# A gated linear recurrence and a low-rank mixer on one core: 96 packed rows for 112, first logarithms summed on TensorE, the sign from bits, and another order

## The chip, the core and the metric

The kernel runs on one core of a Trainium2 chip. The metric is device time in microseconds (us), the median of repeated runs. The core has five engines with queues of their own: TensorE (PE; its weight loads are listed as PEld), VectorE (DVE), ScalarE (ACT), GpSimd (POOL) and SyncE (SP, which issues most DMAs). [...]

## The reference, cut to what matters

```python
# q, k, v, a_re, a_im: (4 batches, 8 heads, 768 steps, 48), float32
mag = np.sqrt(a_re * a_re + a_im * a_im)
scale = np.minimum(mag, 0.999) / (mag + 1e-06)
ar, ai = a_re * scale, a_im * scale
for t in range(S):                       # a state of 48 x 48 complex numbers per head
    new_re = ar[t] * S_re - ai[t] * S_im
    new_im = ar[t] * S_im + ai[t] * S_re
    S_re, S_im = new_re + outer(k[t], v[t]), new_im
    y[t] = q[t] @ S_re
x = y as (4, 768, 384)                   # heads side by side
u = x + (x.transpose(0, 2, 1) @ U @ V).transpose(0, 2, 1)      # rank 32 over the 768 steps
out = u + np.maximum(u @ w_ch1, 0) @ w_ch2                     # 384 -> 1536 -> 384
```

U, V and the two weight matrices come as float64 and are turned into float32 on the chip.

## The kernel before, in words

**Chunks.** Each batch's 768 steps are six chunks of 128, so there are 24 chunks (0 to 23; chunk 5 is the last of the first batch). The complex gates are kept as a logarithm of the magnitude and an angle. Sums of these over the steps of a chunk are products of a 0/±1 matrix with them on TensorE, and exponentials, sines and cosines of the sums turn q and k so that the recurrence becomes products of q with k inside a chunk and a state that goes from chunk to chunk.

**Gates.** Chunks go in groups of two (0 to 11). For a group, `magnitudes_of` (from line 629) takes squares, logarithms and exponentials on ACT and combines them on DVE: `l` is the logarithm of the normalised magnitude, made of two parts, a capped −0.5 ln and a correction `y`. Group 0 is done chunk by chunk (tiles of 384 columns), the others at once (768). `within` sums `l` over the steps (`es ps` and `ef ps`, lines 692 and 696), `of_blocks` over blocks (`tot`, lines 735 and 741). For groups 3 to 11 (`SPLIT`) `l` is split into two rounded parts, `GS`, each with a product of its own in the fp32r format, one record in the trace; for groups 0 to 2 it is one product in float32, which the trace shows as two records. `turns_of` and `angles` (from line 752) make the angle from an arctangent and the sign of a_re. For groups 0 to 2 the sign, times 1/pi, is made on DVE from a_re's bits, and the added 1/4 comes from a product with a constant column; for groups 3 to 11 ACT's Sign function and an Identity with scale 1/pi and bias 1/4 do it (line 384 is the helper through which all activations are recorded; lines 387 and 390 record DVE's products and sums).

**Prep and chain.** `prep` weighs q and k, multiplies them by cosine and sine into `QKC`, per head two parts of 48 columns in 64 each, of which the first 112 of 128 columns are used (48 real, 16 zeros, 48 imaginary), turns them by transposes (line 860, 16 per q or k, in pairs on two halves of the rows) and copies them to `QK` with 112 rows. `chain` scales `QK` by the block totals `T` and takes products over those 112 rows: `inner` (907, 910), `corners` (971), the state's part `dk` (996) and the outputs `y` (1027, 1035), which ACT copies to `xo` (1044, 1046). `T`'s sixteen unused rows are set to one at the start.

**Mixer.** After a batch's six chunks, `mixer` takes two chunks at a time (mixers 0 to 11): rank sums (1070), their spread onto xo (1089), transposes (1107), the products with the first matrix (`up`, 1122; from mixer 7 on `few`, 1222, a scheme with fewer products) and with the second (`down`, 1313 for mixer 0, 1356 from mixer 1 on). Mixer 0's ups are taken before the rank sums are known and put right afterwards (`put_right`, `fix`, 1161). The weights are decoded on DVE and ACT (`single`, 573 to 580).

**Order.** Nothing is scheduled by the compiler. Every operation is first recorded with a kind (such as ("DVE", "gates")); the table `ORDER` then gives each one a place in one global list, found by a planner outside the kernel, and each engine gets its operations in the order of that list. A second table, `SPARE`, gives places at which `idle` (line 1519 records it) puts up to so many blocks of 128 columns of a product of the identity with itself into a PSUM tile that is free at that moment: **filler**, with no use for the result, where the planner expects TensorE to wait.

Of the kernel before, what the change touches and what calls it, by code (L numbers as in the profile page):

```python
# [19 lines left out]
HC = CH // 2  # L20
# [19 lines left out]
        ("POOL", "load"): {0: [14], 1: [34], 1.5: [84], 2: [31]},  # L40
        ("DVE", "load"): {1: [58]},
# [199 lines left out]
def kernel(  # L241
# [19 lines left out]

    nc = tc.nc
    B, H, S, D = q.shape
    DP = 64
    DQ = DP + D
    DM = H * D  # L270
    FF = moe_w_ch1.shape[1]
    R = moe_U.shape[1]
    KD = DM // 128
# [78 lines left out]
    def c_one(n):  # L352
        return 0.15 + 0.00052 * n
# [1235 lines left out]
```

## Time and profile before

| | before |
|---|---|
| median of 3 runs | 628.74 us (627.27 to 629.45) |
| span of the profiled execution | 627.0 us |
| PE / PEld busy | 609.9 / 526.2 us |
| DVE / ACT busy | 499.7 / 415.8 us |
| POOL busy | 38.1 us |
| mean granted TensorE clock | 0.995 |
| filler (line 1519) on PE | 30.6 us |

The span goes from the first to the last instruction of one profiled execution. Busy time of PE is the time in which at least one matmul is under way; an engine's busy time doesn't tell whether its work sets the end. Slices and stages tell more: early stages are about supply, later ones about TensorE's own work.

### The profile page before, as it was taken

The page shows a single profiled execution, that of the slowest core. Times are in us where ns is not written, and L with a number is a line of the kernel's source. Part 1 is how long each engine was busy: PE and PEld are TensorE (multiplying, and loading weights), DVE is VectorE, ACT ScalarE, POOL GpSimd, SP SyncE. Part 2 cuts the span into 40 slices and gives each one's busy share as a digit, 9 for nine tenths or more (in the row PEclk, how much of TensorE's full clock was granted, in tenths as well). Part 3 has the DMA queues.
Part 4 walks back from the last instruction along what each step waited for, and adds up shares of the span by engine and source line. Part 5 has one row for each costly group of instructions (what it writes and reads, how often), then busy time and mean ns, then how long its engine had stood idle before and what let it go on. Part 6 is the DMA issues. An engine that isn't in the chain of part 4 may idle for free.

```text
span 627.0 us, 23447 instructions
## 1 busy us (share of the span) xinstructions
PE 609.9 (97%) x10380; PEld 526.2 (84%) x10380; DVE 499.7 (80%) x887; ACT 415.8 (66%) x807; POOL 38.1 (6%) x79
## 2 busy tenths in 40 slices
PE   6998989999999999999999999999999999999998
PEld 3566767666889889889989989888999998999997
DVE  6899999888999979758977867788989884464554
ACT  6999999999898988687787867688433431202010
POOL 5000000000001010010000100000100100000100
PEclk7999999999999999999999999999999999999999
DMA  8864565644143252541512512601203020000101
GB/s 211 191 146 115 135 136 132 155 111 104 33 80 76 50 120 44 99 89 28 99 37 46 113 40 46 124 19 25 63 21 60 9 51 3 1 1 1 45 14 44
DMA packets 173685, 45.74 MB, mean 73 GB/s; under 512 B 167632, under 2 KB 170384, under 8 KB 173584
## 3 DMA queue, kind: packets, MB, share of 16 engines
q1 hardware_dynamic: 171376, 39.90, 30.1%
q0 software_dynamic: 2208, 4.35, 2.1%
q8 instruction: 81, 1.33, 0.9%
q14 instruction: 20, 0.16, 0.1%
HBM read 33.59 MB, written 4.72 MB: 61 GB/s over the span
## 4 chain that ended last, share of the span: by engine, by line
PE 77%; ACT 4%; DVE 3%; DMA 1%; issue 1%; SPq 0%; ACTq 0%; DVEq 0%
PE down L1356 24%; PE up L1122 15%; PE few L1222 11%; PE dk L996 3%; PE tr L860 3%; PE y L1035 3%; PE inner L910 2%; PE down L1313 2%; PE inner L907 2%; PE tot L741 2%; PE y L1027 2%; PE mixed L1089 2%; PE es ps L692 1%; PE ef ps L692 1%; PE uTp L1107 1%; PE corners L971 1%
## 5 line engine op out<-in xcount | busy, mean ns | idle before, releaser
L1122 PE MATMUL up<-uT,w 128*128 128x256 f32 x504 | 116.9, 383 | 0.0
L387 DVE TENSOR_TENSOR QK<-QK,T 112x512 f32<-112x512 f32 (+2 forms) x144 | 102.1, 732 | 8.4 <-PE inner L910 4.3
L1122 PEld LDWEIGHTS up<-uT,w 128*128 128x128 f32 x504 | 93.6, 190 | 12.5
L1356 PE MATMUL down<-w,h 128*128 128x192 f32 x396 | 72.2, 331 | 0.0
L384 ACT ACTIVATE gate<-gate 128x768 f32<-128x768 f32 (+1 forms) x82 | 64.8, 795 | 7.4 <-DVE GS L791 3.2
L1356 PEld LDWEIGHTS down<-w,h 128*128 128x128 f32 x396 | 64.1, 190 | 1.5 <-issue 0.7
L871 ACT COPY QK<-tr 112x512 f32<-112x512 f32 x96 | 51.2, 590 | 14.6 <-PE tr L860 14.3
L390 DVE TENSOR_TENSOR xo<-down,xo 128x192 f32<-128x192 f32 (+1 forms) x79 | 29.9, 387 | 27.5 <-PE down L1356 27.0
L387 DVE TENSOR_TENSOR QKC<-qk,cs 128x768 f32<-128x768 f32 x44 | 41.7, 955 | 6.3 <-ACT cs L384 3.6
L1230 ACT COPY h<-few 128x512 f32<-128x512 f32 x30 | 17.2, 586 | 40.8 <-PE few L1222 40.8
L1356 PE MATMUL down<-stage 128*128 128x192 f32 x198 | 37.6, 331 | 0.0
L1111 ACT COPY uT<-uTp 128x384 f32<-128x384 f32 x22 | 10.0, 479 | 41.4 <-PE uTp L1107 26.9
L1222 PE MATMUL few<-gate,w 128*128 128x128 f32 x280 | 34.8, 275 | 0.0
L1298 POOL DMA_DIRECT2D out_dram<-xo x32 | 19.2, 644 | 243.3 <-DVE xo L390 140.0
L860 PEld LDWEIGHTS tr<-ident,QKC 64*112 64x112 f32 x768 | 24.5, 130 | 10.7 <-issue 4.7
L1222 PEld LDWEIGHTS few<-gate,w 128*128 128x128 f32 x280 | 33.3, 192 | 0.0
L1356 PEld LDWEIGHTS down<-stage 128*128 128x128 f32 x198 | 32.1, 190 | 0.7 <-issue 0.2
L779 POOL DMA_DIRECT2D gate<-F x15 | 12.0, 799 | 327.9 <-DVE w L578 113.5
L860 PE MATMUL tr<-ident,QKC 64*112 64x64 f32 x768 | 29.4, 221 | 2.3 <-DVE QKC L387 1.6
L381 ACT ACT_TABLE_LOAD x24 | 30.8, 1283 | 1.1 <-PEq L1573 0.7
L384 ACT ACTIVATE h<-up 128x512 f32<-128x512 f32 x42 | 24.6, 596 | 9.8 <-PE up L1122 9.5
L976 ACT COPY AT<-corners 32x128 f32<-32x128 f32 x96 | 24.2, 255 | 9.6 <-PE corners L971 8.3
(200 smaller groups left out, 1285.4 us busy)
## 6 DMA issues: line engine op xcount, KB each, us to landing
stage<-in_moe_w_ch_dram SPq DMA_DIRECT2D x12, 768.0 KB, 5.0
qk<-in_q_dram SPq DMA_DIRECT2D x24, 192.0 KB, 3.2
qk<-in_k_dram SPq DMA_DIRECT2D x24, 192.0 KB, 2.7
VP<-in_v_dram SPq DMA_DIRECT2D x24, 192.0 KB, 3.6
gate<-in_a_re_dram SPq DMA_DIRECT2D x22, 192.0 KB, 3.4
gate<-in_a_im_dram SPq DMA_DIRECT2D x22, 192.0 KB, 3.4
AT<-DG SPq DMA_DIRECT2D x96, 32.0 KB, 2.3
T<-E SPq DMA_DIRECT2D x48, 48.0 KB, 2.9
```

What stands on the lines that cost most here:

```text
L381: ACT(1.37, rank, lambda: nc.scalar.preload_act_table_set(name), writes=[TABLE])
L384: return nc.scalar.activation(out=o, in_=i, func=f, **kw)
L387: nc.vector.tensor_tensor(out=o, in0=a, in1=b, op=OP.mult)
L390: nc.vector.tensor_tensor(out=o, in0=a, in1=b, op=OP.add)
L860: nc.tensor.transpose(out=get(*ps[r])[0:DQ, h], in_=get(*qkc)[at, h].rearrange("p u d -> p (u d)")[:, 0:DQ], identity=ident[at, at], tile_ ...
L871: nc.scalar.copy(out=to, in_=a)
L976: ACT(0.36, RR, lambda r=r, u=u: nc.scalar.copy(out=get(*ATi).rearrange("p (a u) t -> p a u t", u=2)[r:r + BLK, :, u, BLK:2 * BLK], in_=ge ...
L996: nc.tensor.matmul(out=get(*dk[r])[x:end, h], lhsT=get(*ks)[at, h, x // DP, 0:end - x], rhs=get(*VPi)[at, h], start=True, stop=True, tile_ ...
L1122: nc.tensor.matmul(out=get(*ps)[:, e], lhsT=w1[:, f, (ff + e) * 128:(ff + e + 1) * 128], rhs=get(*uT)[:, f], start=(f == 0), stop=(f == KD ...
L1222: nc.tensor.matmul(out=get(*ps)[:, q], lhsT=w()[:, q * 128:(q + 1) * 128], rhs=v[0](), start=(n == 0 and q == 0), stop=True, skip_group_ch ...
L1298: queue.dma_start(out=out[b, c * CH:(c + 1) * CH, lo:hi], in_=get("xo", i)[:, lo:hi])
L1356: nc.tensor.matmul(out=get(*to)[:, part], lhsT=x(j), rhs=y[:, j], start=(first and j == 0), stop=(j == KH - 1), skip_group_check=not first)
```

## The change

1. **96 rows.** `QKC`'s real and imaginary columns stand side by side, 96 per head, with no zeros between; transposes, `QK`, `T` and the states have 96 rows in place of 112. `dk` still takes two products per head and half, of 64 and 48 columns, so that it reads 16 columns of the next head, whose rows in PSUM nobody reads. The memsets of `T` go; those of `QKC` shrink to 32 columns.
2. **Logarithms (groups 0 to 2).** The cap is one DVE pass with one input in all three groups (in groups 1 and 2 it was a Relu on ACT and a two-input pass on DVE), and `l` and `y` are no longer added: each sum takes one product with each of them in the same PSUM tile.
3. **Sign from bits (groups 3 to 11).** Sign on ACT becomes the one-input DVE pass; ACT's Identity goes, and the 1/4 is added while the angle is split into its two rounded parts (ACT's cast gets a bias, DVE's subtraction an added constant).
4. **Order.** `ORDER` and `SPARE` are new throughout: 89 blocks of filler, all of which find a free tile, in place of 153, of which 91 found one. Forty of the 89 stand ahead of the first sum, where there were 8.

The numbers of instructions go from 5664 to 5712 on TensorE, from 887 to 893 on DVE, from 783 to 763 on ACT (24 table loads beside them) and from 79 to 76 on POOL. The diff without `ORDER`, cut to its core:

```diff
-SPARE = {20: 8, 32: 9, 62: 1, 66: 1, 73: 1, 82: 5, 91: 1, 113: 6, 116: 1, 119: 8, 140: 8, 153: 6, 157: 4, 167: 1, 168: 1, 207: 6, 216: 1, 217: 1, 282:
-         1, 352: 2, 436: 1, 514: 5, 518: 5, 527: 4, 546: 4, 547: 25, 551: 12, 596: 2, 601: 1, 606: 3, 624: 1, 632: 3, 646: 1, 653: 1, 664: 1, 672: 2,
-         678: 5, 694: 1, 695: 1, 717: 1, 718: 2}
+SPARE = {30: 40, 83: 6, 95: 3, 107: 10, 115: 4, 142: 6, 148: 2, 223: 5, 260: 7, 265: 2, 578: 2, 601: 2}
...
+    DQ = 2 * D
     DP = 64
-    DQ = DP + D
...
-        QKC.append(singles.tile([128, H, 2, DP], FP, name="QKC%d" % n))
-        nc.gpsimd.memset(QKC[n][:, :, :, D:DP], 0.0)
+        QKC.append(singles.tile([128, H * DQ + DP - (DQ - DP)], FP, name="QKC%d" % n))
+        nc.gpsimd.memset(QKC[n][:, H * DQ:], 0.0)
...
-        nc.gpsimd.memset(TS[n], 1.0)
...
-            if on_dve:
+            if g not in SPLIT:
                 DVE(c_one(W), R1, lambda: nc.vector.tensor_scalar(out=t(l), in0=t(l), scalar1=-0.5, scalar2=-LNMAX, op0=OP.mult,
                                                                   op1=OP.max), [], [L])
-                DVE(cd, R1, lambda: add(t(l), t(l), t(y)), Y, [L])
...
-            if g in BITS:
-                DVE(c_one(W), R1, lambda: nc.vector.tensor_scalar(out=t(n).bitcast(U32), in0=t(ar).bitcast(U32), scalar1=0x80000000,
-                                                                  scalar2=INV_PI, op0=OP.bitwise_and, op1=OP.bitwise_or), AR, [N])
-            else:
-                ACT(ca + 0.09, R1, lambda: act(t(n), t(ar), AF.Sign, bias=tiny), AR, [N])
+            DVE(c_one(W), R1, lambda: nc.vector.tensor_scalar(out=t(n).bitcast(U32), in0=t(ar).bitcast(U32), scalar1=0x80000000,
+                                                              scalar2=INV_PI, op0=OP.bitwise_and, op1=OP.bitwise_or), AR, [N])
...
-                    PE(0.65, R1, lambda: nc.tensor.matmul(out=get(*to), lhsT=m.bitcast(FP), rhs=of(l, i), start=True, stop=True),
-                       [L, name], [to, ("sums", g, i)], takes=[keeps], steps=2)
+                    def two():
+                        for u, a in enumerate((y, l)):
+                            nc.tensor.matmul(out=get(*to), lhsT=m.bitcast(FP), rhs=of(a, i), start=(u == 0), stop=(u == 1))
+                    PE(1.3, R1, two, [L, y + (i,), name], [to, ("sums", g, i)], takes=[keeps], steps=4)
...
-                        nc.tensor.matmul(out=get(*ps)[u * 64:u * 64 + w, p], lhsT=get(*l)[:, h:h + w], rhs=total, start=True,
-                                         stop=True, tile_position=(0, u * 64))
+                        for n, a in enumerate((y, l)):
+                            nc.tensor.matmul(out=get(*ps)[u * 64:u * 64 + w, p], lhsT=get(*a)[:, h:h + w], rhs=total, start=(n == 0),
+                                             stop=(n == 1), tile_position=(0, u * 64))
...
-            if g not in BITS:
-                ACT(ca + 0.09, R2, lambda: act(t(z), t(z), AF.Identity, scale=1.0 / math.pi, bias=fourth), [], Z)
...
-                    ACT(c_act(DM), R2, lambda: nc.scalar.copy(out=of(a, i), in_=of(z, i)), [zi], [a + (i,)])
+                    ACT(c_act(DM) + 0.09, R2, lambda: act(of(a, i), of(z, i), AF.Identity, bias=fourth), [zi], [a + (i,)])
...
-                DVE(c_dve(DM), R2, lambda: nc.vector.tensor_tensor(out=of(b, i), in0=of(z, i), in1=of(a, i).bitcast(FP), op=OP.subtract),
-                    [zi, a + (i,)], [b + (i,)])
+                DVE(c_dve(DM), R2, lambda: nc.vector.scalar_tensor_tensor(out=of(b, i), in0=of(z, i), scalar=0.25, in1=of(a, i).bitcast(FP),
+                                                                          op0=OP.add, op1=OP.subtract), [zi, a + (i,)], [b + (i,)])
...
-                        nc.tensor.transpose(out=get(*ps[r])[0:DQ, h], in_=get(*qkc)[at, h].rearrange("p u d -> p (u d)")[:, 0:DQ],
+                        nc.tensor.transpose(out=get(*ps[r])[0:DQ, h], in_=get(*qkc)[at, h * DQ:(h + 1) * DQ],
                                             identity=ident[at, at], tile_position=(r * HC, 0))
...
-                    for x, end in ((0, DP), (DP, DQ)):
-                        nc.tensor.matmul(out=get(*dk[r])[x:end, h], lhsT=get(*ks)[at, h, x // DP, 0:end - x], rhs=get(*VPi)[at, h],
+                    for x, w in ((0, DP), (DP, D)):
+                        nc.tensor.matmul(out=get(*dk[r])[x:x + w, h], lhsT=get(*ks)[at, h * DQ + x:h * DQ + x + w], rhs=get(*VPi)[at, h],
                                          start=True, stop=True, tile_position=(r * HC, x))
```

(The costs in us inside `PE(...)`, `ACT(...)` and `DVE(...)` are what the planner assumed; the kernel itself does nothing with them.)

More of the change, by code (lines that the diff above doesn't have):

```diff
@@ L30 @@
 ORDER = {
[9 rows of a table removed]
-        ("POOL", "load"): {0: [14], 1: [34], 1.5: [84], 2: [31]},
-        ("DVE", "load"): {1: [58]},
[6 rows of a table removed]
-        ("ACT", "gates"): {0: [1, 2, 4, 6, 7, 16, 17, 22, 23, 29, 28, 45, 70, 71], 1: [24, 27, 38, 39, 41, 42, 46, 47, 65, 64, 67, 68], 2: [129, 108,
[10 rows of a table removed]
-        ("DVE", "gates"): {0: [5, 8, 13, 18, 19, 54, 49], 1: [30, 21, 40, 43, 44, 51, 50], 2: [111, 143, 156, 185, 169], 4: [277, 322, 323, 372, 356],
[10 rows of a table removed]
-        ("ACT", "angles"): {0: [72, 86, 98, 100, 103], 1: [76, 106, 112, 114, 126], 2: [210, 231, 251, 240, 241, 242, 263, 269, 271], 4: [375, 395,
[5 rows of a table removed]
@@ new lines @@
+        ('POOL', 'small'): {0: [884, 1093], 1: [1155, 1018, 1064], 2: [1342, 1377, 1398], 3: [1524, 1468, 1498], 4: [1728, 1771, 1772], 5: [1937,
+        1885, 1957], 6: [2168, 2064, 2127], 7: [2387, 2278, 2289], 8: [2532, 2432, 2515], 9: [2533, 2510, 2564], 10: [2631, 2621, 2640]},
+        ('POOL', 'angles'): {6: [602], 8: [710, 751], 10: [861, 903], 12: [1078], 14: [1246, 1271], 16: [1438, 1474], 18: [1662], 20: [1820, 1862],
+        22: [1990, 2026]},
+        ('DVE', 'mixing'): {7: [1981, 2004, 1995, 2042, 2084, 1986, 1988, 2058, 2067, 2072, 2111, 2117, 2051]},
+}
@@ L301 @@
     PL = H * HC
-    BITS = range(SPLIT[0])
     PUT = (0, 2), (4, 6), (8, 10)
@@ L744, in of_blocks @@
             else:
-                PE(0.51, R1, sums, [l, ("total", 0), ("sums", g)], [ps], way=1, takes=[e], steps=4 * HH)
+                PE(0.82, R1, sums, [l, y + (i,), ("total", 0), ("sums", g)], [ps], way=1, takes=[e], steps=8 * HH)
             used = 2 * D if g in SPLIT else 64 + D
```

45 lines of the change are left out of this document (24 added, 21 removed), and 248 rows, old and new, of the table ORDER.

## The prediction

> **What bounds the kernel now.** I read the page first, for the engines' shares and the slices of the span:
>
> ```profile
> PE 609.9 (97%) x10380; PEld 526.2 (84%) x10380; DVE 499.7 (80%) x887; ACT 415.8 (66%) x807; POOL 38.1 (6%) x79
> PE   6998989999999999999999999999999999999998
> DVE  6899999888999979758977867788989884464554
> ACT  6999999999898988687787867688433431202010
> PEclk7999999999999999999999999999999999999999
> ```
>
> TensorE (PE) is busy for 97% of the 627.0 us, so it looks like the bound. Two things qualify that. Some of the busy time is filler: matmuls of the identity (line 1519), which the order puts in where it expects TensorE to wait. And VectorE (DVE) and ScalarE (ACT) are as full as TensorE in the first quarter. So I cut the span into stages. One limit is the moment at which the output of chunk 5, the last chunk of the first batch, has been copied out, since the rest of mixer 0 hangs on it; the timeline puts it at 117.5 us:
>
> ```profile
> 116.52 0.30 ACT L1044 COPY xo<-y 128x192 f32<-128x192 f32 x1
> 116.84 0.64 ACT L1046 COPY xo<-y 64x192 f32<-64x192 f32 x2
> ```
>
> The busy times by stage (stretch, length, then PE, PEld, DVE, ACT, POOL with counts, granted clock, DMA share, GB/s), and below them the filler's share alone (PE, PEld; its third row is a part of its second):
>
> ```profile
> 0.00:20.00 20.00, 14.13 (x61) 8.38 (x62) 13.62 (x37) 13.21 (x26) 8.41 (x32) 0.83 0.89 212
> 20.00:117.50 97.50, 91.00 (x2152) 67.37 (x2151) 95.56 (x150) 94.05 (x184) 0.00 (x0) 1.00 0.60 140
> 117.50:155.00 37.50, 36.20 (x222) 21.83 (x217) 32.17 (x47) 34.73 (x54) 2.50 (x3) 1.00 0.51 123
> 155.00:600.00 445.00, 444.61 (x7786) 404.92 (x7785) 345.98 (x631) 272.68 (x544) 25.01 (x40) 1.00 0.25 50
> 600.00:627.00 27.00, 23.97 (x169) 23.67 (x167) 12.38 (x26) 1.17 (x2) 2.15 (x4) 1.00 0.10 34
> ```
>
> ```profile
> 0.00:20.00 20.00, 8.89 (x18) 5.05 (x18) 0.83 0.89 212
> 20.00:117.50 97.50, 15.00 (x50) 8.75 (x50) 1.00 0.60 140
> 50.00:117.50 67.50, 1.57 (x6) 0.97 (x6) 1.00 0.57 133
> 117.50:155.00 37.50, 6.71 (x24) 3.90 (x24) 1.00 0.51 123
> ```
>
> The reader is to see three regimes. From 155 to 600 us TensorE never rests (444.61 of 445) and there is no filler: every microsecond of TensorE work there is a microsecond of time, and nothing else is. From 20 to 117.5 us DVE (95.56 of 97.5) and ACT (94.05) are full, while TensorE has 91.0 − 15.0 = 76.0 us of real work: it is fed too slowly. From 117.5 to 155 us TensorE has 36.20 − 6.71 = 29.5 us of real work in 37.5, so it waits 8.0 us, idle or behind filler. The real work is 609.9 − 30.6 = 579.3 us, of which 14.1 − 8.9 + 76.0 = 81.2 lie before 117.5 and 498.1 after it. **The span is thus 117.5 + 498.1 + waits of 8.0, 0.4 and 3.0** (117.5 to 155, to 600, to the end) = 627.0. The prediction replaces each of these terms.
>
> **The change, part by part.** Its single instructions first (line, engine, form, count, busy us, mean ns, idle before):
>
> ```profile
> L384 ACT ACTIVATE GL<-GL,lmax 128x768 f32<-128x768 f32 x10 | 9.3, 930 | 0.1
> L384 ACT ACTIVATE gate<-gate,tiny 128x768 f32<-128x768 f32 x9 | 8.4, 938 | 0.0
> L384 ACT ACTIVATE gate<-gate,fourth 128x768 f32<-128x768 f32 x9 | 8.4, 931 | 2.3 <-DVE gate L760 2.1
> L788 ACT CAST GS<-gate 128x384 fp32r<-128x384 f32 x16 | 8.3, 517 | 1.5 <-DMA gate<-F 1.3
> L384 ACT ACTIVATE F<-ph,magic 128x384 f32<-128x384 f32 x24 | 13.9, 579 | 8.2 <-PE ph L796 7.4 <-PE ph L804 0.4 <-PE ph L801 0.3
> L663 DVE SCALAR_TENSOR_TENSOR GL<-GL,gate 128x768 f32<-128x768 f32 x10 | 9.5, 955 | 3.0 <-ACT gate L384 2.9
> L390 DVE TENSOR_TENSOR GL<-GL,gate 128x384 f32<-128x384 f32 x2 | 1.1, 568 | 0.3 <-ACT gate L384 0.2
> L678 DVE TENSOR_SCALAR gate<-gate 128x768 uint32<-128x768 uint32 x1 | 0.6, 559 | 0.0
> ```
>
> *Sign and fourth (groups 3 to 11).* ACT loses nine Sign (938 ns) and nine Identity (931); its sixteen casts gain a bias, 579 for 517 by the nearest row. DVE gains nine one-input passes of 559. In all ACT −15.8 us, DVE +5.0; the subtraction that now also adds the fourth stays one two-input pass.
>
> *Logarithms (groups 0 to 2).* DVE loses two additions of 568 in group 0; groups 1 and 2 trade a Relu on ACT (930) and a 955 pass on DVE for one of 559. TensorE pays, since each sum now takes two products. The start shows their price (start, length, instruction, count; one product is two records):
>
> ```profile
> 1.42 3.58 PE L1519 MATMUL tr<-ident 128*128 128x384 f32 x6 [1.42 <-POOL ident masks.py:199]
> 8.79 1.62 PE L696 MATMUL es ps<-GL,mid 128*128 128x384 f32 x2 [3.79 <-DVE GL L390]
> 10.21 0.34 PEld L1519 LDWEIGHTS tr<-ident 128*128 128x128 f32 x1 [0.30 <-issue]
> 10.85 0.34 PEld L1519 LDWEIGHTS tr<-ident 128*128 128x128 f32 x1 [0.30 <-issue]
> 15.35 0.81 PE L696 MATMUL es ps<-GL,mid 128*128 128x384 f32 x2
> 16.00 0.81 PE L696 MATMUL ef ps<-GL,fore 128*128 128x384 f32 x2
> 17.69 1.09 PE L735 MATMUL tot<-total,GL 128*64 128x32 f32 x32 [0.66 <-ACT es L384]
> 19.13 1.28 ACT L381 ACT_TABLE_LOAD   x1
> ```
>
> Products of 384 columns follow each other at 0.65 us (15.35 to 16.00), and two chunks' totals take about 1.05. So the twelve sums gain 12 × 0.65 = 7.8 us and the six totals 6 × 0.52 = 3.1: **TensorE +10.9 us, all ahead of 117.5**.
>
> *96 rows for 112.* Rows are the partitions that a product contracts over. The shapes that only lose rows keep their columns, and elementwise passes keep their length per partition, so I cost these at nothing. Only the 768 transposes shrink, their loads from 112 columns to 96:
>
> ```profile
> 97.08 1.08 PE tr L860 x32
> L860 PEld LDWEIGHTS tr<-ident,QKC 64*112 64x112 f32 x768 | 24.5, 130 | 10.7 <-issue 4.7
> L1107 PEld LDWEIGHTS uTp<-ident,xo 128*128 128x128 f32 x72 | 9.0, 141 | 1.0 <-issue 0.4
> ```
>
> Sixteen columns are 11 ns between the last two rows. The transposes go in pairs on two halves of the rows, so 384 pairs save between 0 (load hidden) and 4.2 us; some three quarters lie after 117.5. I take −1.9 there, about the middle, with 0 and −3.2 as ends.
>
> [...]
>
> *The start.* Ahead of the first sum stand now 40 blocks of filler (thirteen products of 384 columns and one of 128) where eight stood; the sum used to wait for the logarithm until 8.79 us. At the cold clock such a product takes 1.28 us (weight loads at 10.21 and 10.85, two per product). Before, the clock was slow until about 14.7, 5.9 us after TensorE took up work at 8.8. If filler from 1.42 on also needs 5.9 us, 4.6 products go cold and 8.7 at 0.65: the first sum starts at 13.2; eight products (5.2) and the totals (2.1) end at 20.5 instead of 18.8. All cold gives 25.8. The chain of angles hangs on this: ACT's exponentials of the totals stand ahead of the table load (19.13), and behind it the first arctangents. ACT's queue is held too, and DVE runs out of weights to decode. I take **+1.5 us**, ends 0 and +7.
>
> [...]
>
> *The order.* Counted through the output of chunk 5, the new order has ahead of it, on DVE: −1.1 (two additions), −0.8 (groups 1, 2), +0.6 (group 3's sign), and pulled forward from later 1.3 (group 3's angle) and 2.5 (one block of w2): net +2.4 us. On ACT: −2.8, and 4.5 pulled forward (three decodes, a table load, one pass of group 3): +1.7. On TensorE: +10.9 and 1.0 pulled forward. DVE is the fuller engine and had 1.9 us idle between 20 and 117.5, so the stage grows by 0.5 to 2.4; I take **+1.5**. TensorE's added 10.9 are covered by its 21.5 us of filler and idleness in that stage and 14.8 in the first 20 us; without that cover they would be on the path (a rival).
>
> What is pulled forward is what pays later. The decode of the weights for mixer 0's last products stands earlier: the first block of w2 by some 30 us of DVE's work, the last block by 5. Only two blocks of filler are placed behind chunk 5's output. In the old order 6.7 us of filler and 1.3 idle lay between 117.5 and 155. In the new one the chain from the batch's rank sums through the correction to the first product of the second matrix still has its hand-offs (TensorE to ACT to TensorE to DVE, some 0.5 each, five of them) with other products between. I take **waits of 3 us for the 8.0**, ends 1 and 8.
>
> *Later.* From 155 us on, ACT (61% busy) has no use for its 15 us; DVE gains about 4 us over 345.98 of 445, hidden as long as no product stands right behind it. The order changes on the queues of SP and POOL are reorderings of the same 287 and 47 transfers. With a DMA share of 0.60 and 0.51 in the two stages that matter I cost them at nothing; in the first 20 us the share is 0.89, and if a load moved back there were late, the decode behind it and DVE's stage would be late by as much. The three memsets gone from POOL end before the first wait there.
>
> **The sum**, against the profiled execution's 627.0 us:
>
> - output of chunk 5: 117.5 + 1.5 + 1.5 = 120.5
> - real TensorE work left: 498.1 − 1.0 (pulled forward) − 1.9 (transposes) = 495.2
> - waits: 3.0 + 0.4 + 3.0 = 6.4
>
> 622.1 us of span. The median of the runs, 628.74, is 1.7 above the profiled span; the same on top gives **623.8 us**, 0.8% faster. With the ends of single terms it spans 620 to 628.
>
> **Rivals.**
>
> *The sums are not hidden (slower).* TensorE's idle and filler time before 117.5 may be hand-offs that stay, with the sums on top, since the exponentials that follow each sum wait for both products. Place: line 696 and 735 between 12 and 80 us; price 10.9 + 1.0. Then chunk 5 is out at 129.4, the span 129.4 + 495.2 + 6.4 = 631.0, the time 632.7. It decides from about 10 us of delay at that output. Against it: DVE and ACT, not TensorE, are full there, and the filler that gives way is larger. For it: of the filler only 1.57 us lie after 50 us, where group 2's third of the sums falls with 5.5 us of idleness to hide it. 0.18.
>
> *The order does not deliver (no change).* The waits between 117.5 and 155 stay at 8.0, because DVE, 86% busy there, hands over late as before: 120.5 + 495.2 + 11.4 = 627.1, time 628.8. For it: DVE has 2.4 us more ahead. Against it: much of that is work taken out of this very stage. 0.16.
>
> *The start costs nothing and the waits go.* The clock is up early, chunk 5 at 118.0, 1 us of waits in place of 8: 118.0 + 495.2 + 4.4 = 617.6, time 619.3. 0.16.
>
> **How the numbers follow.** My forecast gets 0.50, of which 0.46 lies below 626.9 us. A measurement of this kernel tells about 0.3%, or 1.9 us, from no change. Faster by more: 0.46 + 0.16 = 0.62. Within: 0.04 + 0.16 = 0.20. Slower: 0.18. For 8 in 10 the range takes in the forecast, the no-change case and half of the two outer ones: 617 to 632.5; the likeliest case's own range is 620 to 628.
>
> **What would show it.** Right: the copies of chunk 5's output end near 120.5; filler and idleness of TensorE between there and the last product of mixer 0 near 3 us; from then on TensorE full, with under 4 us of waits to the end; 32 transposes in about 1.0 us. The first sum starts near 13 us, the second table load near 20.6. Wrong: chunk 5 past 127 us (sums on the path, or a late start; the rows at 8 to 25 us tell which), new waits of TensorE on DVE after 155 us, or waits of 8 us unchanged in the third stage.

## The result, and the profile after

The changed kernel takes 637.41 us (median of 4 runs, 634.52 to 639.13) beside 629.10 of the kernel before (4 runs, 627.27 to 630.23): a ratio of 1.0131, 95% interval 1.0098 to 1.0164. It is slower, where 623.8 us and "faster" were forecast. The profiled execution has a span of 634.6 us, 12.5 more than the forecast's 622.1.

First the page, its engines and its slices:

```profile
PE 620.2 (98%) x10476; PEld 532.4 (84%) x10476; DVE 499.5 (79%) x893; ACT 401.5 (63%) x787; POOL 35.0 (6%) x76
...
PE   9989989989999999999999999999999999999998
...
DVE  6898979969899979858777968778988877464643
ACT  6989979978888888685786867857333322302020
...
PEclk9999989989999999999999999999999999999999
```

TensorE has 10.3 us more than before (620.2 for 609.9). DVE's row, which had only eights and nines from slice 2 to slice 14, now dips to 7 and 6 in slices 6 and 9 (a slice is 15.9 us), and these are the two slices in which the clock's row has an eight. The stages in the forecast's own stretches say how much (stretch, length, PE, PEld, DVE, ACT, POOL, granted clock, DMA share, GB/s), and below them the filler's part alone:

```profile
0.00:20.00 20.00, 18.58 (x111) 11.54 (x112) 12.82 (x34) 13.10 (x27) 5.17 (x29) 1.00 0.81 198
20.00:117.50 97.50, 92.14 (x2007) 67.25 (x2007) 88.41 (x142) 87.76 (x168) 0.00 (x0) 0.96 0.59 138
...
117.50:155.00 37.50, 35.25 (x404) 21.24 (x393) 31.61 (x48) 31.83 (x56) 0.99 (x2) 0.95 0.54 120
155.00:600.00 445.00, 442.73 (x7749) 401.18 (x7749) 350.53 (x637) 265.34 (x534) 27.80 (x44) 1.00 0.26 52
600.00:634.60 34.60, 31.54 (x231) 31.21 (x229) 16.11 (x35) 3.52 (x6) 1.08 (x2) 1.00 0.06 21
```

```profile
20.00:117.50 97.50, 11.69 (x36) 6.42 (x36) 0.96 0.59 138
```

Between 20 and 117.5 us DVE does 88.41 us of work, where it did 95.56, and ACT 87.76, where it did 94.05: the two full engines of before now stand idle for 9.1 and 9.7 us (1.9 and 3.5 before). The copies of chunk 5's output say the same. They end at 126.3 us, not at 117.5 as before nor at the 120.5 of the forecast:

```profile
125.35 0.31 ACT L1043 COPY xo<-y 64x192 f32<-64x192 f32 x1
125.67 0.32 ACT L1041 COPY xo<-y 128x192 f32<-128x192 f32 x1
126.00 0.32 ACT L1043 COPY xo<-y 64x192 f32<-64x192 f32 x1
```

From there to the end it is 634.6 − 126.3 = 508.3 us, where before had 509.5 and the forecast 501.6. So the miss of 12.5 has two halves: **5.8 us ahead of chunk 5's output and 6.7 behind it.** The experiments take the halves apart. The clock's row shows that TensorE ran at a lower clock for a part of the time (0.50 in three stretches of 3.4 us), but that is not the main part of the loss: one of the four timed runs has a mean granted clock of 1.000 and takes 634.52 us, 5.4 above the 629.10 of before.

### The profile page after: what moved, and what is told of

It is laid out like the page before. It is cut to its first block, busy times and chain, and to the rows that moved or that the text cites. A ratio compares the mean times of both kernels' runs of the same rounds, so it can differ in the third digit from the quotient of the medians.

```text
span 634.6 us, 23648 instructions
## 1 busy us (share of the span) xinstructions
PE 620.2 (98%) x10476; PEld 532.4 (84%) x10476; DVE 499.5 (79%) x893; ACT 401.5 (63%) x787; POOL 35.0 (6%) x76
## 3 DMA queue, kind: packets, MB, share of 16 engines
q1 hardware_dynamic: 171376, 39.90, 30.5%
## 4 chain that ended last, share of the span: by engine, by line
PE 80%; ACT 7%; issue 6%; DMA 3%; DVE 2%; SPq 1%; POOL 0%; another core or an unknown queue 0%; ACTq 0%; POOLq 0%
PE down L1353 23%; PE up L1119 15%; PE few L1219 11%; PE tr L857 3%; PE y L1032 3%; PE dk L993 3%; PE down L1310 3%; PE inner L907 2%; PE y L1024 2%; PE tr L1516 2%; PE inner L904 2%; PE mixed L1086 2%; PE tot L736 2%; DMA gate<-F 1%; PE uTp L1104 1%
## 5 line engine op out<-in xcount | busy, mean ns | idle before, releaser
L1119 PE MATMUL up<-uT,w 128*128 128x256 f32 x504 | 116.8, 384 | 0.0
L384 DVE TENSOR_TENSOR QK<-QK,T 96x512 f32<-96x512 f32 (+2 forms) x144 | 101.7, 726 | 15.5 <-PE corners L968 5.0
L868 ACT COPY QK<-tr 96x512 f32<-96x512 f32 x96 | 50.9, 583 | 14.4 <-PE tr L857 14.4
L1227 ACT COPY h<-few 128x512 f32<-128x512 f32 x30 | 17.3, 588 | 49.7 <-PE few L1219 48.5
L381 ACT ACTIVATE h<-up 128x512 f32<-128x512 f32 x42 | 24.7, 592 | 12.4 <-PE up L1119 12.4
L857 PEld LDWEIGHTS tr<-ident,QKC 64*96 64x96 f32 x768 | 23.9, 123 | 7.7 <-issue 3.8
L919 DVE COPY_PREDICATED DG<-mask,inner 128x128 f32<-128x128 int32 (+1 forms) x72 | 24.0, 341 | 7.5 <-PE inner L904 6.4
L857 PE MATMUL tr<-ident,QKC 64*96 64x64 f32 x768 | 28.5, 220 | 1.1 <-DVE QKC L384 1.0
```

What stands on the lines that cost most here:

```text
L381: return nc.scalar.activation(out=o, in_=i, func=f, **kw)
L384: nc.vector.tensor_tensor(out=o, in0=a, in1=b, op=OP.mult)
L857: nc.tensor.transpose(out=get(*ps[r])[0:DQ, h], in_=get(*qkc)[at, h * DQ:(h + 1) * DQ], identity=ident[at, at], tile_position=(r * HC, 0))
L868: nc.scalar.copy(out=to, in_=a)
L919: nc.vector.copy_predicated(out=to, mask=part(mask[:, n], "p").unsqueeze(1).to_broadcast(list(to.shape)), data=a if t == BLK else a.rearra ...
L1119: nc.tensor.matmul(out=get(*ps)[:, e], lhsT=w1[:, f, (ff + e) * 128:(ff + e + 1) * 128], rhs=get(*uT)[:, f], start=(f == 0), stop=(f == KD ...
```

## The experiments

Sixteen kernels ran beside the two; each was timed against the kernel before on its own chip. "Added" is the real TensorE work (or filler, where it says so) that a kernel has more than before ahead of chunk 5's output, by the prediction's rows; the two right-hand columns are from the one profiled execution of each, so differences of a microsecond in them say little.

| kernel | median us | ratio to before (95%) | added us | chunk 5 out | from there to the end |
|---|---|---|---|---|---|
| before | 627.9 to 629.1 | | 0 | 117.5 | 509.5 |
| changed | 637.4 | 1.0131 (1.0098 to 1.0164) | 10.9 | 126.3 | 508.3 |
| b_rows | 627.8 | 1.0004 (0.9989 to 1.0019) | 0 | 116.8 | 509.1 |
| b_bits | 628.4 | 1.0012 (1.0002 to 1.0023) | 0 | 117.0 | 509.8 |
| b_sums | 636.8 | 1.0146 (1.0129 to 1.0163) | 10.9 | 126.5 | 509.1 |
| b_all | 637.1 | 1.0154 (1.0137 to 1.0171) | 10.9 | 126.2 | 510.1 |
| b_g0 | 632.6 | 1.0049 (1.0032 to 1.0065) | 3.6 | 119.9 | 511.7 |
| b_g12 | 634.8 | 1.0088 (1.0065 to 1.0112) | 7.2 | 121.8 | 510.6 |
| b_drag | 640.9 | 1.0187 (1.0162 to 1.0211) | 11, filler | 127.0 | 511.9 |
| b_sums_swap | 637.7 | 1.0122 (1.0094 to 1.0150) | 10.9, filler −7.3 | 123.2 | 509.9 |
| b_sums_nofill | 639.1 | 1.0151 (1.0131 to 1.0172) | 10.9, filler −11 | 127.9 | 509.8 |
| a_nosums | 635.8 | 1.0100 (1.0073 to 1.0127) | 0 | 126.4 | 509.5 |
| a_fill | 639.7 | 1.0161 (1.0134 to 1.0187) | 10.9 | 128.6 | 509.3 |
| a_shift | 638.7 | 1.0170 (1.0135 to 1.0204) | 10.9 | 127.6 | 509.5 |
| a_fillshift | 638.9 | 1.0156 (1.0134 to 1.0178) | 10.9 | 130.9 | 508.5 |
| mix_to5 | 634.8 | 1.0087 (1.0062 to 1.0113) | 0 | 118.3 | 515.4 |
| mix_5to6 | 635.2 | 1.0094 (1.0066 to 1.0122) | 0 | 116.4 | 515.7 |
| rev_to5 | 641.3 | 1.0213 (1.0170 to 1.0257) | 10.9 | 123.9 | 514.7 |

Names with b_ keep the old order, names with a_ the new one. Theory 1: the sums of groups 0 to 2 are not hidden (the prediction's first rival). Theory 2: the new order costs. A third thought joined them when the changed kernel's trace showed TensorE's clock halved three times: that less filler costs clock.

### One part at a time, in the old order

**b_rows**, the 96 rows and nothing else (the diff's lines on `DQ`, `QKC`, `TS`, `turn` and `state`; `ORDER` untouched):

```diff
+    DQ = 2 * D
     DP = 64
-    DQ = DP + D
```

> The kernel before with the 96 rows alone, in its own order. By the step of my forecast (768 transposes lose 16 columns, taken at 1.9 us after chunk 5 and 0 to 4.2 in all) it is 1 to 3 us below the kernel before, 626 to 628. Theory 1 (the sums of groups 0 to 2 are what costs) and theory 2 (the new order costs) expect the same of it, since both leave the rows out: a time above that of before would make the rows a third cause.

It measures 1.0004: nothing. The loads do get shorter (group row of b_rows; the prediction has 130 ns and 24.5 us for 112 columns):

```profile
L862 PEld LDWEIGHTS tr<-ident,QKC 64*96 64x96 f32 x768 | 24.0, 123 | 10.8 <-issue 4.9
```

Seven ns on a load show, but a group of 32 transposes takes 1.15 us with 96 columns as with 112, chunk 5 comes out only 0.7 us earlier, and the time does not move beyond its interval. Of the two ends that the forecast named for the transposes, 0 (load hidden) is the right one, not the middle that it took.

**b_sums**, two products per sum in groups 0 to 2, with the places of the two additions and two Relus dropped:

```diff
+for _n in (0, 1):
+    del ORDER["DVE", "gates"][_n][4]
+for _n in (2, 4):
+    del ORDER["ACT", "gates"][_n][8]
```

> The kernel before with the sums of groups 0 to 2 as two products each, in its own order (the places of the two additions and two Relus dropped). Theory 1, the 10.9 us of TensorE work go on the path because what I counted as its cover is hand-offs: chunk 5's output 6 to 9 us later than in before, the time 635 to 638. Theory 2, the cost comes from the new order's hand-offs and late loads: the sums hide in TensorE's idle and filler time, 627 to 631.

1.0146, or 9.0 us, at the upper end of theory 1. The sums alone, in the old order with all of its filler, make the kernel as slow as the whole change does. The stage and the waits of DVE and ACT in it (who waited for whom: us, times, longest), all of kernel b_sums:

```profile
20.00:117.50 97.50, 93.02 (x2068) 69.14 (x2064) 86.60 (x139) 86.21 (x164) 0.00 (x0) 0.96 0.56 129
```

```profile
DVE gate L768 <- ACT gate L390: 3.5, 2, 1.9
DVE QKC L393 <- PE dk L1004: 1.6, 1, 1.6
DVE w L393 <- ACT w L390: 1.5, 1, 1.5
```

```profile
ACT E L390 <- PE tot L743: 3.1, 5, 0.8
...
ACT gate L390 <- PE ef ps L703: 1.2, 2, 0.8
```

The longest waits of DVE and of ACT in the same stage of before were these:

```profile
DVE DG L922 <- PE inner L907: 0.9, 1, 0.9
```

```profile
ACT E L384 <- PE tot L741: 0.7, 1, 0.7
```

With two products per sum ACT waits for totals and sums (`E` for `tot`, `gate` for `ef ps`), and DVE waits for ACT behind it: TensorE's added time has become theirs.

**b_bits**, the sign from bits in groups 3 to 11, the DVE pass standing where ACT's Sign stood:

```diff
+for _n in range(6, 24, 2):
+    ORDER["DVE", "gates"][_n].append(ORDER["ACT", "gates"][_n].pop(11 if _n == 6 else 12))
+    del ORDER["ACT", "angles"][_n][1]
```

> The kernel before with the sign from bits in groups 3 to 11, in its own order: DVE gains 5 us, ACT loses 16, nearly all of it after 117 us where both have slack. Theory 1 and theory 2 both expect no change, 628 to 630. A time over 632 would mean that DVE's added passes stand on the path, a third cause.

1.0012, at most 1.4 us by its interval, so no part of the loss that counts, as both theories said. **b_all** joins the three:

> All three changes of the computation in the order of before, with its filler. Theory 1: as the changed kernel or a little below it, 633 to 637. Theory 2: near or below the kernel before, 625 to 630, and the difference to the changed kernel's 637 is the order's.

1.0154, as the changed kernel. Its granted clock is full from 20 us to chunk 5's output, so the clock is not needed for the loss:

```profile
20.00:117.50 97.50, 91.31 (x2088) 67.26 (x2084) 87.58 (x144) 85.59 (x163) 0.00 (x0) 1.00 0.56 129
```

Against b_rows (116.8) the sums put chunk 5's output back by 9.4 of their 10.9 us.

**b_g0 and b_g12** split the sums by group, two products where `g in TWO` and one elsewhere:

```diff
+    TWO = (0,)        # b_g12: (1, 2)
...
+                        parts = (y, l) if g in TWO else (l,)
+                        for u, a in enumerate(parts):
```

> The kernel before with two products per sum in group 0 alone (TensorE +3.6 us, DVE -1.1, within the first 20 us). If every added microsecond of TensorE counts alike, a third of the 9.0 us: 630.5 to 631.5. If the filler and idleness of the first 20 us hide it, 627 to 629, and groups 1 and 2 carry all of the cost.

> The kernel before with two products per sum in groups 1 and 2 alone (TensorE +7.2 us; ACT -1.9, DVE -0.8). Group 0 alone cost 3.7 us and all three groups 9.0. If the costs add up, 5.3: 633.5 to 635. If the TensorE time between 20 and 60 us hides group 1's part once group 0 is short again, 631 to 632.

Group 0 costs 3.7 us by the medians (2.0 to 4.1 by the ratio's interval) for 3.6 added, even in the first 20 us, where TensorE was idle or on filler most of the time; groups 1 and 2 cost 5.9 (4.1 to 7.0) for 7.2. Together 9.6, beside 9.0 measured at once: within the intervals the costs add up, and no group's part is hidden. Not all of it shows at chunk 5's output, which comes 2.4 and 4.3 us later; in b_g0 another 2.2 us come behind it, and their cause stays open.

### A dose of TensorE time, and filler taken out

**b_drag** computes as before. Behind the last totals of groups 0, 1 and 2 it has 17 blocks of filler each, 51 in all (11 us at 0.65 us for three):

```diff
+for _at in (73, 207, ORDER["PE", "rest"][2][3]):
+    SPARE[_at] = SPARE.get(_at, 0) + 17
```

> The kernel before, computing as before, with 17 blocks of filler (3.65 us) added right behind the last totals of each of the groups 0, 1 and 2: the same TensorE time as the sums add (10.9 us), but no exponential waits for it. If it is TensorE's throughput that is short there, nearly the same loss as with the sums, 634 to 637. If it is the longer wait of ACT's exponentials for their sums, 628 to 631, with the filler hidden.

1.0187, 12.0 us, more than the sums themselves. By the trace the filler ahead of chunk 5's output grows from 23.9 to 34.9 us, and that output comes 9.5 us later. Nothing waits for these products, and yet the stage reads like that of b_sums (kernel b_drag, stage and DVE's waits):

```profile
20.00:117.50 97.50, 91.71 (x1993) 66.33 (x1991) 85.96 (x137) 85.12 (x163) 0.00 (x0) 1.00 0.55 127
```

```profile
DVE GM L391 <- PE y L1039: 5.9, 2, 3.4
DVE F L811 <- ACT F L388: 3.6, 2, 3.4
```

DVE waits 3.4 us in one go, nearly one dose of 3.65, for products that stand behind the dose in TensorE's queue. So it isn't the longer wait of the exponentials in particular: **TensorE time added at these places is paid, useful or not, by whoever waits for the next product in the queue.**

**b_sums_nofill** and **b_sums_swap** ask whether the filler can make room:

```diff
+for _at in [n for n in SPARE if 70 < n < 300]:      # b_sums_nofill
+    del SPARE[_at]
...
+for _at, _less in ((82, 5), (113, 6), (119, 6), (140, 1), (153, 6), (157, 4), (207, 6)):      # b_sums_swap
+    SPARE[_at] -= _less
```

> Two products per sum in groups 0 to 2, the order of before, and 51 of its 90 blocks of filler (those between about 19 and 59 us, 11 us at full clock) left out. If filler that stands in TensorE's queue ahead of products which others wait for passes the delay on, 629 to 634. If the hand-offs alone set the pace there, no change from the 636.8 us with the filler; if the filler holds up the clock, above 638 and a granted clock under 0.9 between 20 and 60 us.

> Two products per sum in groups 0 to 2, the order of before, and 34 blocks of its filler (7.3 us at full clock) left out around the sums of groups 0 and 1, so that the added products stand in for it (7.2 us of theirs belong to these groups). If filler time there is time to spare, as my prediction took it, chunk 5 is out near 119.5 instead of 126.5 and the time is 629 to 631. If the filler only showed the waits of a chain in which TensorE's real products take their turn, the sums lengthen that chain and nothing comes back: chunk 5 near 126, 635 to 638.

Without the filler nothing is won: 1.0151, where b_sums has 1.0146, with a mean granted clock of 0.979 over the profiled execution and 0.72 between 20 and 50 us. There the filler holds up the clock, which is 1.00 in the same stretch of b_sums. The swap's time (1.0122, six runs from 633.2 to 639.3, the granted clock from 0.999 down to 0.992) cannot be told from that of b_sums. Its profiled execution, one of the quicker ones at full clock, has chunk 5 out at 123.2, 3.0 ahead of b_all's 126.2 at full clock. Of 7.3 us of filler taken out, 3.0 come back; that is between the two answers expected, and neither of them.

### The new order

**a_nosums** gives the changed kernel its additions back:

```diff
+for _n, _y in ((0, 6), (1, 5)):
+    _d = ORDER["DVE", "gates"][_n]
+    _d.insert(4, max(_d[3], ORDER["ACT", "gates"][_n][_y]) + 0.5)
+for _n in (2, 4):
+    _a, _d = ORDER["ACT", "gates"][_n], ORDER["DVE", "gates"][_n]
+    _a.insert(8, _a[7] + 0.25)
+    _d[2] = max(_d[2], _a[8]) + 0.5
```

> The changed kernel, its order and filler kept, with the logarithms of groups 0 to 2 added on ACT and DVE again (one product per sum; the additions get places right behind what they need). The sums alone in the old order cost 9.0 us. If the sums are the whole cost and the new order neither gains nor loses, 627 to 630; if the new order gains what I forecast of it and the sums ate that gain, 621 to 625; if the new order only works with the short DVE chain, 632 or more.

1.0100, in the range of the last of the three answers. Chunk 5 comes out at 126.4 though 10.9 us of TensorE work are gone. So theory 1 is not the whole story either: **taking the sums out of the new order does not make it fast.** In the old order the sums cost 9 us; in the new one 1.6 (less than the intervals tell apart), on a base that is 7 us slower. Why it is slower this run alone does not tell, since the additions stand at places put in by hand. But two things stand in its trace that before hardly has. One is idle time of TensorE in the midst of a group of products, with nothing that it waits for ("issue"):

```profile
46.77 0.49 PE L1039 MATMUL y<-GM,QK 96*64 96x48 f32 x9
49.63 0.43 PE L1039 MATMUL y<-GM,QK 96*64 96x48 f32 x7 [2.37 <-issue]
```

Nine of sixteen products, 2.37 us of nothing, then the other seven. The stalls of 0.15 us and more add up to 5.0 ahead of chunk 5 in a_nosums and 2.8 in the changed kernel; before has one of 1.05 us. The other is the clock: three times in the changed kernel, and twice in a_nosums, it is halved for 3.4 us, during a stall or wait or within some 2 us behind one. In the changed kernel:

```profile
45.80:49.20 3.40, 3.40 (x40) 2.26 (x36) 1.93 (x2) 2.55 (x7) 0.00 (x0) 0.50 0.57 175
86.80:90.20 3.40, 3.03 (x6) 1.76 (x7) 2.09 (x2) 2.15 (x6) 0.00 (x0) 0.50 0.83 186
131.10:134.50 3.40, 3.40 (x22) 0.89 (x16) 3.17 (x4) 2.32 (x4) 0.00 (x0) 0.51 0.67 130
```

Half the clock for 3.4 us is 1.7 us of work. In a_nosums the stalls and the two stretches come to 8.4 us (1.05 in before), most of the 8.9 by which its chunk 5 is late; so it is not shown that the new order's hand-offs are slow by themselves.

**a_fill** and **a_shift** try the two, **a_fillshift** both:

```diff
+SPARE[185], SPARE[601] = 8, 7      # a_fill
...
+SPARE[30] = 32                     # a_shift, with 32 products of 32 columns ahead of the 32 blocks
+        if run == 32:
+            for _ in range(32):
+                idle(1, 32)
```

> The changed kernel with 13 blocks of filler more: 8 ahead of the second totals of group 1 (where TensorE idles 1.56 us at 43.3) and 5 more ahead of the fold of the rank sums (1.15 us at 127.8). Behind these two gaps its clock is halved for 3.4 us each. If the half clock costs what it takes from the products (1.7 us each), 633.5 to 635.5 and a granted clock of 1.00 from 45 to 50 and from 130 to 135; if TensorE is not what others wait for there, no change from the 637.4 of the changed kernel.

> The changed kernel with 32 small products (32 columns) at its very start in place of 8 blocks of filler, which moves every later instruction of TensorE back by about 116 in its queue and leaves the work alone. TensorE's stalls in the midst of a group of products (2.15 us at 85.0, no wait shown) have so far stood at every 256th instruction. If they come from the queue's own supply of instructions, they move to other products, at the same count, and the 2.15 us shrink or grow: 634 to 637. If they come from the corner products themselves, the stall at the corners of chunk 3 stays.

> Both edits of the two runs before, in the changed kernel. If the half clock and the stall each cost what they seem to, 631 to 634; this would still be slower than the kernel before (628 to 629), by what the sums and the order's other waits cost. If neither counts, 637.

None is faster than the changed kernel (the intervals overlap), and each misses its expected time. In a_fill the first clock gap is gone (granted clock 1.00 from 45 to 50 us) and chunk 4 is out at 121.2 instead of 122.2, but then the disturbance falls elsewhere (stretches of a_fill):

```profile
45.00:50.00 5.00, 5.00 (x180) 4.27 (x180) 3.15 (x5) 3.76 (x8) 0.00 (x0) 1.00 0.31 79
...
117.50:130.00 12.50, 11.23 (x187) 7.11 (x182) 9.59 (x16) 8.47 (x17) 0.96 (x1) 0.62 0.60 114
```

With a clock of 0.62 over 12.5 us and a new stall of 0.86 us in them (until 121.2), what was won is lost again. So a_fill doesn't price the clock, and it stays open what the changed kernel would take with no stall and no half clock. a_shift did settle what the stalls go with, a count of instructions; that is told in the last section.

### Old order up to chunk 5, new order behind it, and the other way round

These kernels give every operation its old place if it comes ahead of chunk 5's output (rev_to5: its new place), and the other order's place behind that. Their edits are whole tables `ORDER` and `SPARE`; the places p in them follow these rules:

```python
p = x if x < 585 else 10000 + y                                  # mix_to5: x the old place, y the new
p = x if x < 585 else 10000 + y if y < 900 else 20000 + x        # mix_5to6
p = y if y < 597.5 else 10000 + x                                # rev_to5
```

> 96 rows and sign from bits, one product per sum; the old order through chunk 5's output, and everything behind it in the changed kernel's relative order with its filler. Chunk 5 should be out at 117 as in before. If the gain between chunk 5 and 6 is the later order's own, chunk 6 is out near 179 (183.3 in before) and the time 623 to 626, the new order's later waits (2.2 us between 200 and 270 us) included. If that gain was bought with weight decoding pulled forward ahead of chunk 5, chunk 6 stays at 182 or later and the time is 627 to 632.

> As mix_to5, but the changed order is used only from chunk 5's output to about chunk 7's, and the old relative order behind that, so that the waits between 200 and 270 us should be gone. If the gain between chunk 5 and 6 is the later order's own: 621 to 624, faster than both kernels. If it was bought ahead of chunk 5: 626 to 630.

> All three changes of the computation; the changed kernel's order and filler through chunk 5's output, the old relative order behind it. Chunk 5 out near 126.5. If the gain between 5 and 6 was bought ahead, chunk 6 is at 188.5 and, without the later waits, the time 632 to 635. If it is the later order's own, 636 to 639.

None of the expected times came. Each seam made a wait of its own (waits of TensorE between 110 and 200 us, first of mix_to5, then of rev_to5; mix_5to6 has 3.9 us where mix_to5 has 3.7), and about it the clock is halved for 6.8 us in all three:

```profile
PE rT L1019 <- ACT r L959: 3.7, 1, 3.7
```

```profile
PE mixed L974 <- DVE rw L1023: 2.7, 1, 2.7
```

At the seam of mix_to5 the products that the new order would put between the rank sums and their fold are presumably already done. The new order's gain behind chunk 5 was not had on top of the old order's first stage in this way; whether it can be in another is open. But rev_to5 gives one number of use. Up to chunk 5 it is the changed kernel operation by operation, and in its profiled execution the clock stayed up:

```profile
20.00:117.50 97.50, 92.20 (x2108) 68.09 (x2106) 90.92 (x147) 90.69 (x173) 0.00 (x0) 1.00 0.60 141
```

Chunk 5 is out at 123.9 there, 2.4 us ahead of the changed kernel's profiled 126.3, with stalls of 2.0 us in sum for 2.8. So about 2.4 of the 8.8 us by which chunk 5 is late are half clock and longer stalls, and 6.4 are there at full clock, the 2.0 us of stalls among them. That is less than the 8.7 of b_all: by these two profiles, both at full clock, the new order hides more of the sums than the old one does, and not enough of them.

## Why the prediction was wrong, step by step

**What bounds the kernel: right as a reading, wrong as a budget.** DVE and ACT were full, TensorE was not. From this the prediction drew that "TensorE's added 10.9 are covered by its 21.5 us of filler and idleness in that stage and 14.8 in the first 20 us". **This is the step that failed.** With 81.2 + 10.9 + 1.0 = 93.1 us of real work ahead of chunk 5's output, an output at 120.5 needs filler and idle time to shrink from 36.3 to 27.4 us there. The profiled executions show what they did (us from the start to that output; "idle" is TensorE not busy):

| kernel | until | filler | idle | both | real work |
|---|---|---|---|---|---|
| before | 117.5 | 23.9 | 12.4 | 36.3 | 81.2 |
| forecast | 120.5 | | | 27.4 | 93.1 |
| b_all (old order) | 126.2 | 23.6 | 11.0 | 34.6 | 91.6 |
| b_sums_swap (old order, less filler) | 123.2 | 15.4 | 15.0 | 30.4 | 92.8 |
| changed | 126.3 | 22.9 | 7.2 | 30.1 | 96.2 |
| rev_to5 (new order, full clock) | 123.9 | 23.5 | 7.0 | 30.5 | 93.4 |

So the cover was 1.7 us in the old order and 6.2 in the new, where 8.9 were counted on. Filler took its time wherever the order put it (b_drag's added 11 us show in full, 34.9 us for 23.9), and the new order has 22.9 us of it ahead of that output, hardly less than the old one's 23.9. Where filler was taken out (b_sums_swap, 8.2 us less than b_all by these rows), half came back as idle time. What is then added pushes whatever is next in the queue (b_sums 9.0 us, b_drag 12.0 with products that nobody needs, b_g0 3.7 for 3.6).

**The price of the sums was right**: between before and b_all the real work up to chunk 5's output grows by 10.4 us, where 10.9 were taken. In the changed kernel TensorE's busy time grew by 10.3 us with 7.0 less filler (23.6 for 30.6), so its real work by 17.3. Of that 10.9 are the sums, as worked out, and some 5.1 the three stretches at half clock (3.4 us each, of which half is lost); 1.3 are not placed. The start went better than forecast, and shows the products 0.65 us apart:

```profile
11.81 0.81 PE L690 MATMUL es ps<-gate,mid 128*128 128x384 f32 x2
12.46 0.81 PE L690 MATMUL es ps<-GL,mid 128*128 128x384 f32 x2
...
18.84 0.28 PE L730 MATMUL tot<-total,GL 128*64 128x32 f32 x4
```

```profile
19.51 1.28 ACT L378 ACT_TABLE_LOAD   x1
```

The first sum starts at 11.81, not 13.2, and the table load at 19.51 against 19.13 before: +0.4 us, where +1.5 was taken. The forecast had taken the warm-up of 5.9 us that it read from the trace of before. In the changed kernel's trace the weight loads of the filler stand 0.64 us apart up to 4.79 us, 3.4 after the filler's start at 1.42, and 0.32 apart from there on. Why before took 5.9 us from 8.8 on is open.

**The order, ahead of chunk 5: +1.5 was too small.** The net counts per engine did not tell it. By the table, 126.3 − 120.5 = 5.8 is 2.7 us of filler and idle time that did not give way and 3.1 us by which TensorE's own work is longer than counted; two stretches at half clock before that output are worth 3.4, a term that the prediction had at nothing. At full clock (rev_to5) 3.4 us are left, with 2.0 us of stalls in them. The first rival had the sums on the path and chunk 5 at 129.4; it was given 0.18.

**The loads, costed at nothing, have a part in this.** Before, the loads of a_re between 20 and 60 us are issued at 22.84 and 30.29 us, and ACT waits for no load from 20 to 117.5. In the changed kernel they are issued at 28.48 and 39.51, and ACT waits for the second of them until 43.18:

```profile
ACT gate L381 <- DMA gate<-in_a_re_dram: 2.1, 1, 2.1
```

```profile
PE tot L730 <- ACT h L381: 1.6, 1, 1.6
```

ACT's pass `h` stands behind that wait in its queue, and the totals of group 1 wait for `h`: TensorE idles until 44.84, and at 45.8 the first stretch at half clock begins. In rev_to5 ACT waits 0.85 us for the same load, and the clock stays up. No run moves this load alone, so its share of the time is not known.

**Waits between 117.5 and 155 us, 8.0 to 3.0: right in sign.** From chunk 5's copies to chunk 6's the changed kernel takes 188.6 − 126.3 = 62.3 us, before 65.8, b_all 65.6. That is 3.3 to 3.5 gained, where about 6 were forecast (5.0 of waits, 1.0 pulled forward). TensorE's wait for the rank sums is 1.15 us, and behind it the spread of the rank sums runs at half clock (timeline of the changed kernel):

```profile
128.99 0.85 PE L1133 MATMUL rT<-fold,r 64*128 64x32 f32 x6 [1.15 <-ACT r L1073]
...
130.80 4.47 PE L1142 MATMUL rw ps<-w,rw 128*32 128x512 f32 x24 [0.19 <-DVE rw L1135]
```

**"Later: no new waits" was wrong.** From 200 to 270 us TensorE is busy for 67.79 of 70 us, with full clock; b_all, with the same computation in the old order, for 69.97. First the changed kernel, then b_all:

```profile
200.00:270.00 70.00, 67.79 (x1516) 59.91 (x1519) 61.14 (x105) 55.09 (x111) 3.35 (x5) 1.00 0.44 85
```

```profile
200.00:270.00 70.00, 69.97 (x1522) 62.20 (x1520) 61.38 (x106) 56.95 (x114) 2.86 (x5) 1.00 0.40 79
```

Some 1.5 of these 2.2 us are waits for ACT, by the trace, and all of them give back about two thirds of what the stage before gained. The last stretch has 34.6 − 31.54 = 3.1 us of waits, as forecast (3.0).

**The transposes** gained nothing measurable (b_rows, 1.0004), where 1.9 us were taken. **DVE's added passes** in groups 3 to 11 were hidden, as forecast (b_bits).

Of the 6.7 us behind chunk 5 some 2.5 are thus waits that stayed (half clock included), 2.2 new waits and 1.9 transposes. What is not settled: the losses do not add up (sums 9.0 in the old order, order about 7, both 8.3), so no single share can be given to each, and the order's part may be stalls, half clock and late loads rather than its hand-offs. Shown is that the sums alone in the old order, and the new order without the sums, are each about as slow as the whole change (1.0146 and 1.0100 beside 1.0131), and that the rows and the bits are not.

## What to carry to other kernels

Here TensorE's idle and filler time was not room that added work could count on: with 8.2 us of filler less, b_sums_swap had 15.0 us of idle time for b_all's 11.0, and added work was paid by whoever waited for the next product in the queue (DVE in b_drag, 3.4 us in one go). Before counting on such cover, add a dose of useless work at the very places and time it: here 11 us of it cost 12. And when an order is planned anew around a part, test the order without that part too, since both can cost alone and hide each other together, and look at the first wait for each load that was moved back.

## What the runs showed of the hardware that was not expected

**TensorE's stalls stand at the same counts of instructions.** The stalls marked "issue" stand at the same counts of instructions in different kernels. Up to the stall, the changed kernel and a_shift have executed the same number (stretches from 0 to just before the stall, x is the count; changed kernel, then a_shift, then before):

```profile
0.00:87.10 87.10, 80.77 (x1491) 55.42 (x1491) 73.72 (x132) 72.87 (x137) 5.17 (x29) 0.98 0.67 156
0.00:103.50 103.50, 96.87 (x1743) 66.98 (x1744) 87.70 (x152) 87.36 (x166) 5.17 (x29) 0.97 0.64 149
```

```profile
0.00:84.85 84.85, 78.60 (x1491) 55.25 (x1491) 72.07 (x129) 73.11 (x137) 5.16 (x29) 1.00 0.67 157
```

```profile
0.00:96.80 96.80, 84.46 (x1743) 58.58 (x1744) 88.99 (x154) 88.32 (x169) 8.41 (x32) 0.96 0.65 154
```

1491 products and 1491 loads in both, though a_shift moved other products there: the changed kernel stalls within the corners, a_shift at the same count within the outputs, as the first of its two answers expected.

```profile
84.56 0.45 PE L968 MATMUL corners<-QK 96*32 96x32 f32 x31
87.17 0.26 PE L968 MATMUL corners<-QK 96*32 96x32 f32 x1 [2.15 <-issue]
```

```profile
84.91 0.49 PE L1035 MATMUL y<-GM,QK 96*64 96x48 f32 x10 [1.21 <-issue]
```

Another stall of the changed kernel (0.35 us at 103.6) and the only one of before (1.05 us) share a count too (1743 and 1744), and b_rows stalls at the same product as before (0.78 us, behind the 55th of 64 `inner`). From 2982 to 3487 it is 505 recorded instructions, twice about 253. The third stall of the changed kernel (0.31 us at 69.6) stands at 1109 and 1110, 763 ahead of 2982, three times 254; a_shift's next (1.59 us until 119.93) at 2253 and 2253, 1524 behind it, six times 254. That is near the "every 256th instruction" of a_shift's expectation, but not every such count has a stall. The page of the changed kernel has a queue that it calls "instruction":

```profile
q8 instruction: 82, 1.34, 0.9%
```

82 packets of 16 KB, beside 20952 recorded matmuls and weight loads of TensorE, about 256 of them to a packet; before has 81 for 20760, a_shift 83 for 21068. That is close to the 252 to 254 of the stalls; that a stall is the wait for a late packet is not shown. The longest stall lasts 2.37 us (a_nosums), and those printed here stand among small products (`inner`, `corners`, `y`). In the changed kernel the data queue is full meanwhile (101.0% of its time between 82.4 and 87.2 us):

```profile
q1 hardware_dynamic: 3904, 0.84, 101.0%
```

But it is at 82% around the 2.37 us of a_nosums (46.0 to 49.6) and at 43% around the 1.05 us of before (93 to 96.8), so that full queues are the reason is not shown.

**Short gaps can go with a halved clock.** In the changed kernel three gaps of TensorE, of 1.56, 2.15 and 1.15 us, each have a stretch of 3.4 us at a granted clock of 0.50 with them, which begins between 0.4 us before the gap's end and 2.2 us behind it. The length of a gap alone does not decide it: at 1.05 us in before (until 96.84), 1.50 us in rev_to5 (until 86.5) and 1.60 us in b_drag (until 407.3) the clock stayed up (1.00 from 20 to 117.5, from 50 to 117 and from 270 to 600 us), and in b_sums it was halved from 95.7 to 102.5 us (0.79 from 90 to 100, 0.93 from 100 to 117.5) with no gap over 0.8 us in the six microseconds before. What decides is open.
